# Two shared side tiles to the end, second hidden in the block sums' space, and a new order

## The chip, the cores and the metric

The kernel runs on one core of a Trainium2 chip. The core has TensorE (PE, matmuls and weight loads), VectorE (DVE), ScalarE (ACT), GpSimd (POOL) and a queue (SP) that starts the DMAs. PE writes to PSUM, eight banks of 128 x 512 f32. The metric is device microseconds of one execution; the median of 3 runs of the kernel before is 963.83 (962.95 to 963.94).

## What is computed

```python
scores = (q @ k.T) / sqrt(64)          # B=8, H=8, S=576, D=64
scores = where(block_i >= block_j, scores, -1e9)   # blocks of 64
attn   = softmax(scores) @ v
x      = attn.transpose(0, 2, 1, 3).reshape(4608, 512)
out    = relu(x @ w_in) ** 2 @ w_out   # w_in 512x2048, w_out 2048x512
```

All is f32 to the caller. Both large products run in f16: each operand is split into a high and a low f16 part, and three matmuls (high x high, high x low, low x high) make one product.

## The kernel before

The work is cut into 4048 tasks with names; every instruction is issued by one helper, so all rows of a trace have line 331 and are told apart by their tiles.

**Attention.** 40 "passes" of two heads each (i = 0 to 39). Passes 0 to 7 take only the first rows, 8 to 15 the rest of the same heads, 16 to 39 all rows. A full pass has three groups of rows. For each group: `A` scores on PE into a side tile (two PSUM banks), `B` the row maximum on DVE (`nmx`, read from the side tile), `C` the exponential on ACT (`p`, read from the side tile, which is free behind it), `S` and `R` row sums and inverses, `H` and `L` the f16 high and low parts of the probabilities (`p_rows`), `T` a DMA that transposes them (`p_turned`). Then `G` multiplies with v on PE (`px`) and `X` evicts `px` to x.

**The rest.** x is taken in 12 chunks of 384 tokens in the order 0, 1, 2, 4, 3, 5, 7, 6, 8, 10, 9, 11. A chunk is normed (`nq`, `hb`, `xm`) and split to f16 (`xt_all`). The first three chunks go in 16 units each: `ph` (12 matmuls of 128x384 into `pair`), then `pos`, `sqr`, `top`, `rem` (relu, square, high, low), the result in `hidden`. The other nine go in four groups each, of seven products of blocks (`p1 p2 p6 p5 p7 p4 p3`, 12 matmuls of 128x192 each) into two PSUM banks X and B, read by `c11`, `a11` and so on into `r`; `p3` is the last product, `a12` its reader on DVE. The groups need sums of blocks of w_in (`t0_0` to `t3_17`, in `turned_w`). Behind each chunk come the output products `po{chunk}_{m}_{f}` (three matmuls of 128x512, 48 per m) with the eviction `ob` and the store. The weights come as int64 words (`r` raw w_in, `z` raw w_out); `bits`, `prelu`, `join`, `max`, `cast` and `low` make scaled f16 parts of them.

**The order.** One string, `ORDER`, lists all tasks in the order in which they are issued, with a letter for the engine where there is a choice (`D`, `A`, `P`). `Plan.run` issues them, and each engine's queue keeps that order. `Plan.add` says what a task needs, which ring of buffers it takes a slot of, and which it frees.

**PSUM.** Before pass 14 (`ALONE`): side0 and side1 (two banks each), pair0 and pair1 (a bank each), and `ps_x`, two banks for everything that is called `x`, `px` among it. From pass 14 on side1 and pair1 are given up for three banks `group`, a ring of three for the groups' X and B. Output products of late chunks take pair0 alone (`po`). The raw pieces of w_out lie where `PLACES` says, in parts of `w2`, `hidden` and `turned_w`.

Of the kernel before, what the change touches and what calls it, by code (L numbers as in the profile page):

```python
# [8 lines left out]
F32 = mybir.dt.float32  # L9
# [8 lines left out]
PSUM = bass.MemoryType.PSUM  # L18
# [90 lines left out]
D7:P F5:A nq0_0 bits0_7 C8_1 E6 F6:A bits0_5 w0d0 w0e0 E7 F7:A r13 r14 G4 keys10 X4_0:A clear join0_4 hb0_0 S8_1 G5 cast0_0:A D8_0:A X5_0:A G6 join0_6
A9_0 xm0_0 G7 X6_0:A Q4:A bits0_11 E8_0_0 h0_0 X7_0:A R8_1 low0_0 max0_11 B9_0 Q6:A bits0_8 Q5:A cast0_1:P E8_0_1 Q7:A F8_0_0:A bits0_13 max0_14 nq1_0  # L110
max0_12 prelu0_7 max0_8 C8_2 F8_0_1:A hb1_0 load10 join0_5 load8 D8_1:A max0_9 S8_2 E8_0_2 F8_0_2:A R8_2 A9_1 E8_1_0 xm1_0 bits0_9 l0_0 C9_0 h1_0 B9_1
D8_2:A E8_1_1 l1_0 bits0_10 F8_1_0:A F8_1_1:A max0_13 A9_2 E8_2_0 E8_2_1 z0 prelu0_8 r15 max0_15 z1 F8_2_0:A F8_2_1:A join0_7 z2 z3 bits1_0 prelu0_9
S9_0 R9_0 C9_1 D9_0:A w0a1 prelu0_10 ph0_0 w0b1 low0_1 cast0_2:P B9_2 w0c1 join0_8 G8_1 low0_2 S9_1 R9_1 C9_2 join0_9 w0d1 ph0_1 prelu0_11 cast0_3:A
w0e1 bits0_12 w0e A10_1 D9_1:A bits1_3 A10_0 ia0_0 E9_0_0 bits1_1 pos0_0 low0_3 prelu0_12 join0_10 S9_2 join0_11 R9_2 cast0_4:P pos0_1 z4 B10_0 X8_1:A
bits0_14 F9_0_0:A sqr0_1 D9_2:A low0_4 join0_12 ph0_2 prelu0_13 top0_1:D pos0_2 prelu0_14 C10_0 E9_0_1 cast0_5:P ph0_3 E9_0_2 F9_0_2:A B10_1 ph0_4
F9_0_1:D bits1_2 C10_1 pos0_3 low0_5 E9_2_0 S10_0 bits0_15 join0_14 R10_0 prelu0_15 join0_13 D10_0:D cast0_6:P sqr0_3 prelu1_0 pos0_4 low0_6 prelu1_1
keys11 join1_0 cast0_7:P A10_2 E9_1_0 F9_1_0:A A11_0 S10_1 join0_15 sqr0_0 B10_2 F9_2_0:A low0_7 ph0_5 cast0_8:P E9_2_1 prelu1_2 top0_0:D B11_0
max1_0:A ph0_6 top0_3:A pos0_5 join1_2 R10_1 C10_2 S10_2 low0_8 E9_1_1 F9_2_1:A rem0_3 ph0_7 R10_2 F9_1_1:A cast0_9:D load9 A11_1 sqr0_4 G9_1 rem0_1
z5 low0_9 B11_1 D10_1:A sqr0_2 pos0_7 bits1_5 pos0_6 cast0_10:P C11_0 D10_2:D low0_10 load11 prelu1_3 E10_0_0 sqr0_5 S11_0 top0_2:D X9_1:A F10_0_0:A
C11_1 E10_0_1 top0_5:D max1_2:D join1_1 load12 cast0_11:P F10_0_1:A E10_0_2 F10_0_2:A R11_0 sqr0_7 max1_1:D bits1_4 S11_1 sqr0_6 A11_2 E10_1_0  # L120
F10_1_0:A load13 E10_1_1 A12_0 low0_11 z6 top0_4:D cast0_12:P z7 E10_2_0 B11_2 F10_1_1:A R11_1 join1_3 rem0_4 prelu1_4 max1_3:D D11_0:A low0_12 ph0_8
top0_7:A C11_2 F10_2_0:A E10_2_1 F10_2_1:A rem0_0 prelu1_5 D11_1:A join1_4 ph0_9 pos0_9 cast0_13:P B12_0 A12_1 prelu1_6 G10_1 S11_2 C12_0 pos0_8 z8
prelu1_7 join1_5 R11_2 max1_5:A rem0_7 X10_1:A A12_2 E11_0_0 D11_2:D low0_13 B12_1 cast0_14:P F11_0_0:A max1_4:D vals12 ph0_10 C12_1 B12_2 E11_0_1
E11_0_2 bits1_6 join1_6 A13_0 low0_14 S12_1 F11_0_1:A prelu1_8 max1_6:D F11_0_2:A sq0_1_0 bits1_7 join1_7 S12_0 bits1_8 rem0_2 R12_1 join1_8 E11_2_0
# [273 lines left out]
def attention_moe_kernel(ctx: ExitStack, tc: tile.TileContext, qk1, v1, qk, ks, vm, vt, w_in, w_out, out):  # L398
# [387 lines left out]
    def side_of(t, group):  # L786


        if t["i"] >= ALONE:
            return 0  # L790
# [1233 lines left out]
```

## Time and profile before

| | before |
|---|---|
| median of 3 runs | 963.83 us |
| the profiled execution | 963.4 us |
| its span | 961.6 us |
| PE busy | 936.5 us, 97% |
| DVE busy | 764.7 us, 80% |
| ACT busy | 638.6 us, 66% |
| POOL busy | 267.9 us, 28% |

The span is what the profile covers; 1.8 us of the execution lie outside it. A busy PE is not yet PE at its best: its rows overlap by the pipeline's depth, so how fast matmuls go is read from start to start. PE's idle time is short and lies in few places, so a table by stretches is read first, and then the timelines of these places. Rows of DVE and ACT matter where PE waits for them.

### The profile page before, as it was taken

What the parts mean: (1) busy time and instruction counts of PE and PEld (TensorE: products, weight loads), DVE (VectorE), ACT (ScalarE), POOL (GpSimd) and SP (SyncE); (2) the same over time, 40 slices, a digit from 0 to 9 for tenths busy, and PEclk for the clock granted to TensorE, in tenths of its full rate; (3) what the DMA queues carried; (4) which work ended last, traced back from release to release, by engine and by line L of the source; (5) the groups of instructions that cost most, each with busy time, mean ns of one, the idle gap of its engine ahead of it and who ended that gap; (6) DMA issues with size and microseconds to landing.
All of it is one profiled execution on the core that took longest, in us unless ns stands there. A gap on an engine that the chain in (4) does not pass through costs nothing.

```text
span 961.6 us, 21188 instructions
## 1 busy us (share of the span) xinstructions
PE 936.5 (97%) x8145; PEld 602.6 (63%) x8145; DVE 764.7 (80%) x1703; ACT 638.6 (66%) x1585; POOL 267.9 (28%) x371
## 2 busy tenths in 40 slices
PE   8899899999998999999999999999999999999998
PEld 5455444545554784785676675686675675596675
DVE  6999997789899997899879788698879777656331
ACT  6999986765895786885475576678657555365330
POOL 4586401222255541224032032031112012011110
PEclk9999999999999999999999999999999999999999
DMA  9915477656855318435665346564473354400001
GB/s 358 399 63 186 153 163 164 139 135 136 188 115 121 83 51 190 104 63 118 124 155 123 78 107 112 119 150 94 86 176 84 74 117 81 91 13 12 12 1 45
DMA packets 221650, 114.93 MB, mean 120 GB/s; under 512 B 195290, under 2 KB 203756, under 8 KB 221548
## 3 DMA queue, kind: packets, MB, share of 16 engines
q1 hardware_dynamic: 221548, 113.57, 48.5%
q8 instruction: 64, 1.05, 0.4%
q14 instruction: 38, 0.31, 0.1%
HBM read 58.21 MB, written 9.46 MB: 70 GB/s over the span
## 4 chain that ended last, share of the span: by engine, by line
PE 81%; DVE 10%; ACT 3%; POOL 2%; issue 2%; DMA 2%; SPq 0%; DVEq 0%; ACTq 0%; POOLq 0%
PE pair L331 40%; PE group L331 24%; PE side L331 8%; PE px L331 6%; DVE nmx L331 2%; DVE p_rows L331 2%; PE po L331 2%; DVE w L331 2%; DMA w<-in_w_in 1%; POOL w L331 1%; DVE xt_all L331 1%; DVE stw L331 1%; DMA vraw<-in_v 1%; ACT p L331 1%; DVE x L331 1%
## 5 line engine op out<-in xcount | busy, mean ns | idle before, releaser
L331 PE MATMUL pair<-w,hidden 128*128 128x512 f16 (+1 forms) x1680 | 382.1, 376 | 1.0 <-DVE ob L331 0.9
L331 PEld LDWEIGHTS <-hidden 128*128 128x128 f16 x1776 | 168.5, 98 | 179.0 <-issue 11.7
L331 PEld LDWEIGHTS <-w 128*128 128x128 f16 x2304 | 200.4, 98 | 56.9 <-issue 10.3
L331 ACT ACTIVATE p<-side,nmx 128x576 f32<-128x576 f32 (+8 forms) x264 | 140.1, 541 | 94.3 <-DVE nmx L331 45.6
L331 POOL TENSOR_TENSOR hidden<-r,hidden 128x384 f16<-128x384 f32 x103 | 104.0, 1020 | 219.7 <-ACT hidden L331 204.6
L331 PE MATMUL group<-xt_all,w 128*128 128x192 f16 x1728 | 161.8, 247 | 0.8 <-DVE xt_all L331 0.5
L331 DVE SCALAR_TENSOR_TENSOR p_rows<-p,rs,p_rows 128x64 f16<-128x64 f32 (+7 forms) x264 | 147.2, 578 | 11.0 <-ACT p_rows L331 8.8
L331 DVE TENSOR_REDUCE nmx<-side 128x1 f32<-128x192 f32 (+8 forms) x288 | 123.4, 481 | 27.2 <-PE side L331 26.4
L331 POOL TENSOR_SCALAR sm<-sm 128x2 f32<-128x2 f32 (+2 forms) x104 | 34.5, 332 | 333.2 <-ACT p L331 316.0
L331 PE MATMUL group<-xt_all,turned_w 128*128 128x192 f16 x1296 | 122.8, 246 | 0.0
L331 PEld LDWEIGHTS <-turned_w 128*128 128x128 f16 x1296 | 108.1, 98 | 14.2 <-issue 4.9
L331 ACT ACTIVATE p_rows<-p,rs 128x64 f16<-128x64 f32 (+11 forms) x173 | 90.3, 554 | 31.8 <-DVE rs L331 21.2
L331 ACT ACTIVATE r<-group,rescale 128x384 f32<-128x384 f32 x111 | 63.7, 579 | 69.2 <-PE group L331 61.5
L331 ACT ACTIVATE r<-r 128x384 f32<-128x384 f32 x177 | 90.9, 523 | 20.0 <-DVE r L331 17.7
L331 ACT CAST hidden<-r 128x384 f16<-128x384 f32 x172 | 84.7, 507 | 28.8 <-DVE r L331 19.1
L331 DVE SCALAR_TENSOR_TENSOR r<-group,rescale,r 128x384 f32<-128x384 f32 x108 | 65.9, 613 | 45.8 <-PE group L331 32.5
L331 PE MATMUL side<-qk 64*64 64x512 f32 (+2 forms) x480 | 97.0, 498 | 3.5 <-ACT p L331 3.4
L331 PE MATMUL pair<-xt_all,w 128*128 128x384 f16 x576 | 98.9, 326 | 1.1 <-DVE xt_all L331 0.7
L331 PE MATMUL side<-ks,qk 64*64 64x192 f32 (+4 forms) x576 | 91.9, 424 | 0.0
L331 PE MATMUL px<-p_turned,v 128*64 128x384 f16 (+5 forms) x1168 | 66.8, 269 | 0.3 <-ACT p_turned L331 0.3
L331 PEld LDWEIGHTS <-v 128*64 128x64 f16 x1128 | 48.5, 110 | 21.5 <-issue 11.3
L331 DVE TENSOR_TENSOR hidden<-r,hidden 128x384 f16<-128x384 f32 x89 | 51.3, 579 | 7.5 <-ACT hidden L331 7.1
(154 smaller groups left out, 1060.3 us busy)
## 6 DMA issues: line engine op xcount, KB each, us to landing
qk<-in_qk SPq DMA_DIRECT2D x32, 576.0 KB
ks<-in_ks SPq DMA_DIRECT2D x32, 320.0 KB
vraw<-in_vm SPq DMA_DIRECT2D x30, 256.0 KB
w<-in_w_out SPq DMA_DIRECT2D x10, 512.0 KB
out<-ob SPq DMA_DIRECT2D x17, 256.0 KB
w<-in_w_in SPq DMA_DIRECT2D x8, 512.0 KB
out<-ob SPq DMA_DIRECT2D x26, 128.0 KB
hidden<-in_w_in SPq DMA_DIRECT2D x6, 512.0 KB
```

The lines of the kernel that those rows point to most:

```text
L331: i = make(*a, **k)
```

## The change

`ps_x`, the `group` banks and the switch at pass 14 go. The eight banks are now side0, side1, pair0, pair1, single0, single1 from the start to the end. Scores take the two side tiles in turn through one ring `s`, and the products with v of passes from 16 on (and others that aren't "whole") take a whole side tile of the same ring, one half for each of their two parts. The groups' X and B take pair0 and pair1, swapped from group to group. single0 and single1 are the ring `x` early on; later single0 is `y` (norms, v's scales), single1 is `po`. The second chunk's hidden lies in `turned_w`'s space, so the block sums from `t{n}_3` on come only after the second chunk's output products with those parts. `PLACES` puts other raw pieces of w_out in turned_w. `ORDER` is new as a whole, with other letters too: of the weights' casts ACT has 14 for 12, DVE 10 for 7, POOL 8 for 13; of the row sums DVE 36 for 29, POOL 12 for 19; of the high parts of p_rows ACT 167 for 155, DVE 97 for 109. PE's matmuls are the same in number and shape.

```diff
 PLACES = (
     {f: ("w2", 7 - f) for f in range(8)} | {f: ("hidden", f - 8) for f in range(8, 14)} | {14: ("turned", 0), 15: ("turned", 1)},
-    {0: ("w2", 7), 1: ("w2", 6), 2: ("w2", 5), 4: ("w2", 4)}
-    | {5: ("w2", 7), 6: ("w2", 6), 7: ("w2", 5), 9: ("w2", 7), 10: ("w2", 6), 11: ("w2", 7)}
-    | {3: ("turned", 2), 8: ("turned", 3), 12: ("turned", 4)},
+    {3: ("w2", 7), 4: ("w2", 6), 5: ("w2", 5), 6: ("w2", 4)}
+    | {7: ("w2", 7), 8: ("w2", 6), 9: ("w2", 7), 10: ("w2", 6), 11: ("w2", 7)}
+    | {0: ("turned", 2), 1: ("turned", 3), 2: ("turned", 4)},
 )
...
-p0 A0 B0 C0 p1 A1 A2 B1 S0 R0 C1 r0 max0_0 prelu0_0 B2 D0:P S1 R1 C2 r1 prelu0_1 bits0_0 A3 p2 D1:P E0 F0:A A4 r2 B3 C3 E1 max0_1 A5 bits0_1 S2
+p0 p1 r0 r1 p2 A0 r2 r3 A1 r4 B0 C0 p3 B1 r5 C1 S0 A2 R0 r6 D0:D r7 max0_0 prelu0_0 A3 S1 r8 bits0_0 R1 B2 r9 D1:P E0 prelu0_1 keys8 B3 C2 r10 bits0_1
...
-    ps_x = ctx.enter_context(tc.tile_pool(name="ps_x", bufs=2, space=PSUM))
-    sides = [ps_b.tile([P, 1024], F32, name="side0")]
-    pairs = [ps_b.tile([P, 512], F32, name="pair0")]
-    early = ExitStack()
-    ps_e = early.enter_context(tc.tile_pool(name="ps_e", bufs=1, space=PSUM))
-    sides.append(ps_e.tile([P, 1024], F32, name="side1"))
-    pairs.append(ps_e.tile([P, 512], F32, name="pair1"))
-    homes = {"mm": pairs, "po": pairs[:1]}
-    turns_of = dict(mm=0, po=0, g=0)
+    bank = lambda name, n: ps_b.tile([P, 512 * n], F32, name=name)
+    pairs, singles = ([bank(f"{name}{n}", 1) for n in range(2)] for name in ("pair", "single"))
+    homes = {"s": [bank(f"side{n}", 2) for n in range(2)], "mm": pairs, "x": singles, "y": singles[:1], "po": singles[1:]}
+    turns_of = {ring: 0 for ring in homes}
...
-        if ring not in homes:
-            early.close()
-            ps_g = ctx.enter_context(tc.tile_pool(name="ps_g", bufs=1, space=PSUM))
-            homes[ring] = [ps_g.tile([P, 512], F32, name=f"group{n}") for n in range(3)]
         turns_of[ring] += 1
         return homes[ring][(turns_of[ring] - 1) % len(homes[ring])]
...
+    hidden_too = turned_w.rearrange("p i z b k -> p (i z b k)").rearrange("p (f z s) -> p f z s", f=NF, z=2)
...
-            ps = box["ps"] = sides[side_of(t, group)]
+            ps = box["ps"] = bank_of("s")
...
-        full = ps_x.tile([P, 512], F32, tag="x", name=f"px_{u}_{g}")
+        if t["whole"]:
+            full = bank_of("x")
+        else:
+            if "home" not in t:
+                t["home"] = bank_of("s")
+            full = t["home"][:, 512 * (1 - g) :]
...
+    def hidden_of(ck):
+
+        return hidden_too if turn_of.index(ck) == 1 else hidden
...
         def bank(name):
-            box[name] = bank_of("g")[:, :CH]
+            box[name] = pairs[(g + (name == "B")) % 2][:, :CH]
...
-            {"s0": 1, "s1": 1, "mm": 2, "x": 2, "p32": 2, "ks": 2, "v16": 2, "g": 3, "po": 1, "qk": 2, "r": 8, "hb": 2, "ob": 3, "dg": 1, "top": 1}
+            {"s": 2, "mm": 2, "x": 2, "y": 1, "p32": 2, "ks": 2, "v16": 2, "g0": 1, "g1": 1, "po": 1, "qk": 2, "r": 8, "hb": 2, "ob": 3, "dg": 1, "top": 1}
...
-                    ("p1", lows("01") + weights + ([f"p2{ck}_{g - 1}"] if g else []), ("g",)),
-                    ("p2", [f"p1{k}"], ("g",)),
+                    ("p1", lows("01") + weights + ([f"p2{ck}_{g - 1}"] if g else []), (f"g{g % 2}",)),
+                    ("p2", [f"p1{k}"], (f"g{1 - g % 2}",)),
...
-                add(f"a12{k}", "DVE", 545, [f"p3{k}", f"c12{k}"], r, step("a12"), frees=[(f"p2{k}", "g")])
+                add(f"a12{k}", "DVE", 545, [f"p3{k}", f"c12{k}"], r, step("a12"), frees=[(f"p2{k}", f"g{1 - g % 2}")])
...
+                if x == 3:
+                    after += [f"po{turn_of[1]}_{m}_{4 * n + e}" for m in range(3) for e in range(4)]
...
-                        f"G{i}", "PE", 2186 if len(gs) > 1 else 1844, back + [f"vl{i}"], rank + 6, both_parts, ("x",) * len(gs),
+                        f"G{i}", "PE", 2186 if len(gs) > 1 else 1844, back + [f"vl{i}"], rank + 6, both_parts, ("s",),
```

How the order moves, at three places. First PE at the last group of scores of pass 21 and the first of pass 22 (`qk_1`, `qk_2` and `ks_1`, `ks_2` are queries and keys of these groups, `side` their tile). Before, some 100 rows lie between the two:

```order
L331 MATMUL pair_76<-w_108,hidden 128x512
L331 MATMUL side_75<-qk_1_0_3202 64x512 x2
L331 MATMUL side_75<-ks_1_0_3204 64x64 x2
L331 MATMUL side_75<-ks_1_0_3204,qk_1_0_3202 64x448 x2
L331 LDWEIGHTS v_3_0_0_3464
...
L331 MATMUL pair_76<-w_108,hidden 128x512
L331 MATMUL side_75<-qk_2_0_3693 64x320 x2
L331 MATMUL side_75<-ks_2_0_3695,qk_2_0_3693 64x256 x2
L331 MATMUL side_75<-qk_2_0_3693 64x64 x2
L331 MATMUL side_75<-ks_2_0_3695,qk_2_0_3693 64x192 x2
```

After, in the same place:

```order
L331 MATMUL single_75<-w_104,hidden 128x512
L331 MATMUL side_77<-qk_1_0_2963 64x512 x2
L331 MATMUL side_77<-ks_1_0_2965 64x64 x2
L331 MATMUL side_77<-ks_1_0_2965,qk_1_0_2963 64x448 x2
L331 MATMUL side_76<-qk_2_0_3517 64x320 x2
L331 MATMUL side_76<-ks_2_0_3519,qk_2_0_3517 64x256 x2
L331 MATMUL side_76<-qk_2_0_3517 64x64 x2
L331 MATMUL side_76<-ks_2_0_3519,qk_2_0_3517 64x192 x2
L331 LDWEIGHTS turned_w
```

The two groups used one tile with other work between them; now they stand back to back and have a tile each.

Second DVE at the same place (`nmx` is the row maximum of those scores, `p_rows` the low parts of pass 20's probabilities). Before:

```order
L331 SCALAR_TENSOR_TENSOR p_rows<-p_3_1_0_7_3604,rs_1_0_7_3718,p_rows 128x128
L331 TENSOR_SCALAR m_2_0_3734<-pm_2_0_3646 128x2
L331 TENSOR_TENSOR turned_w<-t_AluOpType.subtract_3639,turned_w 128x2x256
L331 SCALAR_TENSOR_TENSOR p_rows<-p_3_1_0_7_3604,rs_1_0_7_3718,p_rows 128x384
L331 SCALAR_TENSOR_TENSOR p_rows<-p_3_1_0_7_3604,rs_1_0_7_3718,p_rows 128x512
L331 TENSOR_REDUCE nmx_1_0_8_3748<-side_75 128x1 x2
L331 TENSOR_SCALAR nmx_1_0_8_3748<-nmx_1_0_8_3748 128x2
```

After:

```order
L331 TENSOR_SCALAR ob_1_3724<-single_75,uv_3466 128x512
L331 TENSOR_REDUCE nmx_1_0_8_3739<-side_77 128x1 x2
L331 TENSOR_SCALAR nmx_1_0_8_3739<-nmx_1_0_8_3739 128x2
L331 TENSOR_TENSOR t_AluOpType.subtract_3756<-w_103 128x512
L331 SCALAR_TENSOR_TENSOR p_rows<-p_3_1_0_7_3656,rs_1_0_7_3685,p_rows 128x128
L331 TENSOR_REDUCE nmx_2_0_4_3770<-side_76 128x1 x4
L331 TENSOR_SCALAR nmx_2_0_4_3770<-nmx_2_0_4_3770 128x4
L331 TENSOR_TENSOR xt_all<-x_93,xt_all 128x768
L331 SCALAR_TENSOR_TENSOR p_rows<-p_3_1_0_7_3656,rs_1_0_7_3685,p_rows 128x384
```

The row maximum stood behind the two wide lows of `p_rows`; now both row maxima stand ahead of them.

Third PE at the hand-over from the third to the fourth group of chunk 4 (`group` and `pair` are the groups' banks, the weights are parts of `xt_all`). Before, the next group's first product, into `group_3837`, stands ahead of the old group's last, into `group_3839`:

```order
L331 LDWEIGHTS turned_w
L331 MATMUL group_3838<-xt_all,turned_w 128x192
L331 LDWEIGHTS w_107
L331 MATMUL group_3837<-xt_all,w_107 128x192
...
L331 LDWEIGHTS w_107
L331 MATMUL group_3839<-xt_all,w_107 128x192
```

After, one output product stands between the last matmul of the old group's last product and the next group's first:

```order
L331 LDWEIGHTS w_103
L331 MATMUL pair_73<-xt_all,w_103 128x192
L331 LDWEIGHTS hidden
L331 MATMUL single_75<-w_104,hidden 128x512
...
L331 LDWEIGHTS w_103
L331 MATMUL pair_73<-xt_all,w_103 128x192
```

There were three banks in turn, so the next group opened a free one; now it opens the bank `pair_73` that the old group has just filled.

## Rows read from the trace of the kernel before

**Rows 1.** The page: span, and each engine's busy time.

```profile
span 961.6 us, 21188 instructions
PE 936.5 (97%) x8145; PEld 602.6 (63%) x8145; DVE 764.7 (80%) x1703; ACT 638.6 (66%) x1585; POOL 267.9 (28%) x371
```

**Rows 2.** Stretches: us, busy PE, PEld, DVE, ACT, POOL, clock, DMA share, GB/s.

```profile
0.00:20.00 20.00, 15.21 (x143) 11.19 (x145) 13.06 (x51) 13.81 (x54) 9.09 (x23) 1.00 0.91 346
20.00:120.00 100.00, 88.62 (x658) 50.28 (x655) 95.69 (x205) 94.75 (x236) 61.70 (x82) 0.97 0.58 209
120.00:300.00 180.00, 180.00 (x1315) 92.90 (x1314) 157.58 (x359) 130.76 (x327) 48.10 (x67) 1.00 0.66 147
300.00:320.00 20.00, 16.88 (x156) 11.18 (x155) 18.31 (x30) 11.25 (x27) 10.74 (x11) 0.91 0.49 90
320.00:820.00 500.00, 498.85 (x4753) 339.54 (x4751) 417.73 (x945) 333.61 (x835) 118.22 (x169) 1.00 0.50 110
820.00:961.60 141.60, 136.95 (x1134) 97.56 (x1128) 62.33 (x118) 54.38 (x108) 20.09 (x22) 1.00 0.13 30
```

**Rows 3.** Timeline of PE, 303 to 318: start, us, what, [idle before, releaser].

```profile
303.06 0.65 PE L331 MATMUL side<-qk 64*64 64x512 f32 x2
...
311.58 0.49 PE L331 MATMUL side<-qk 64*64 64x320 f32 x2 [3.07 <-ACT p L331]
...
312.50 1.24 PE L331 MATMUL pair<-w,hidden 128*128 128x512 f16 x3
313.52 3.44 PE L331 MATMUL group<-xt_all,w 128*128 128x192 f16 x24
316.80 1.15 PE L331 MATMUL group<-xt_all,turned_w 128*128 128x192 f16 x12
```

**Rows 4.** Timelines of POOL, DVE and ACT at the same place.

```profile
305.11 2.92 POOL L331 TENSOR_TENSOR _AluOpType.subtract<-_AluOpType.subtract,w 128x512 f32<-128x512 f32 x2
...
305.50 3.08 DVE L331 SCALAR_TENSOR_TENSOR p_rows<-p,rs,p_rows 128x384 f16<-128x384 f32 x2
308.50 1.27 DVE L331 TENSOR_REDUCE nmx<-side 128x1 f32<-128x576 f32 x2
...
310.08 0.74 ACT L331 ACTIVATE p<-side,nmx 128x576 f32<-128x576 f32 x1 [2.97 <-DVE nmx L331]
```

**Rows 5.** Groups by line and form, DVE: busy, mean ns of one | idle before.

```profile
L331 DVE SCALAR_TENSOR_TENSOR p_rows<-p,rs,p_rows 128x512 f16<-128x512 f32 x28 | 22.6, 806 | 0.0
...
L331 DVE SCALAR_TENSOR_TENSOR p_rows<-p,rs,p_rows 128x384 f16<-128x384 f32 x28 | 19.1, 682 | 1.1 <-ACT p_rows L331 1.0
```

**Rows 6.** Timeline of PE, two groups of scores in one side tile.

```profile
156.19 0.65 PE L331 MATMUL side<-qk 64*64 64x512 f32 x2
...
157.22 3.41 PE L331 MATMUL pair<-w,hidden 128*128 128x512 f16 x15
160.56 0.65 PE L331 MATMUL side<-qk 64*64 64x512 f32 x2
```

**Rows 7.** Timeline at 350: last product into a group's bank, and its reader.

```profile
350.72 1.40 PE L331 MATMUL group<-xt_all,w 128*128 128x192 f16 x15
...
352.16 0.62 DVE L331 SCALAR_TENSOR_TENSOR r<-group,rescale,r 128x384 f32<-128x384 f32 x1 [0.30 <-PE group L331]
```

**Rows 8.** Groups by line and form: the weights' casts on three engines.

```profile
L331 POOL TENSOR_SCALAR w<-w,wsc 128x512 f16<-128x512 f32 x12 | 22.7, 1893 | 14.0 <-DVE w L331 13.7
...
L331 DVE TENSOR_SCALAR w<-w,wsc 128x512 f16<-128x512 f32 x7 | 3.4, 481 | 0.1
...
L331 ACT ACTIVATE w<-w,wsc 128x512 f16<-128x512 f32 x11 | 7.9, 719 | 4.2 <-DVE w L331 4.1
```

**Rows 9.** Timelines of DVE and PE at 826: one output bank in turn.

```profile
826.05 0.81 DVE L331 TENSOR_SCALAR ob<-pair,uv 128x512 f32<-128x512 f32 x1 [0.98 <-PE pair L331]
...
826.92 1.45 PE L331 MATMUL pair<-w,hidden 128*128 128x512 f16 x6 [0.90 <-DVE ob L331]
```

**Rows 10.** Timeline of DVE at the end.

```profile
957.89 0.54 DVE L331 TENSOR_SCALAR ob<-pair,uv 128x256 f32<-128x256 f32 x1 [3.65 <-PE pair L331]
```

More of the change, by code (lines that the diff above doesn't have):

```diff
@@ L109 @@
[L109 to L112, printed above, removed]
@@ L709, in turned @@
         def turned():
-            pm = box["pm"] = ps_x.tile([P, 512], F32, tag="x", name=f"pm_{u}")
+            pm = box["pm"] = bank_of("x" if pair[0]["i"] == WHOLE else "y")
             nc.tensor.transpose(pm[:2, :P], box["st"], ident)
@@ L784, in scores @@
                 nc.tensor.matmul(ps[D * h : D * h + D, o], q[rs], keys[rs, k], start=True, stop=True)
-    def side_of(t, group):
-        if t["i"] >= ALONE:
-            return 0
-        n = [j for g, _, _ in t["groups"] for j, _ in g[:1]].index(group[0][0])
-        return (t["i"] * len(t["groups"]) + n) % 2
     def rows(t, group):
@@ L1361, in products @@
                 ring = out_ring(ck, n)
-                bank = ps_x.tile([P, 512], F32, tag="x", name=f"po_{ck}_{n}") if ring == "x" else bank_of(ring)
-                box["po"] = bank[:, :w]
+                box["po"] = bank_of(ring)[:, :w]
             for i, (z, k) in enumerate(((0, 0), (0, 1), (1, 0))):
@@ L1618, in norm @@
             step = lambda n: lambda *q: box["s"][n](*q)
-            add(f"hb{k}", "DVE", 680 if big == 1 else 950, frees, rank, start, ("hb",), frees=[(f"nq{k}", "x")])
+            add(f"hb{k}", "DVE", 680 if big == 1 else 950, frees, rank, start, ("hb",), frees=[(f"nq{k}", x_of_norm(b, g))])
             add(f"xm{k}", "DVE", 160 + 0.985 * size, [f"hb{k}"], rank, step("scaled"), frees=[(f"hb{k}", "hb")])
@@ L1688, in square @@
             add(
-                f"nq{k}", "PE", 165 * len(halves), [f"sa{k}_{a}" for a in halves], rank, sums, ("x",),
+                f"nq{k}", "PE", 165 * len(halves), [f"sa{k}_{a}" for a in halves], rank, sums, (x_of_norm(b, g),),
                 frees=[(f"sq{k}_{a}", "sq") for a in halves],
@@ L1740, in moe @@
                 add(f"a22{k}", "DVE", 545, [f"p5{k}", f"c22{k}"], r, step("a22"))
-                add(f"a12{k}", "DVE", 545, [f"p3{k}", f"c12{k}"], r, step("a12"), frees=[(f"p2{k}", "g")])
-                add(f"c21{k}", {"ACT": 469, "DVE": 533}, 0, [f"p4{k}"], r, step("pos"), ("r",), frees=[(f"p1{k}", "g")])
+                add(f"a12{k}", "DVE", 545, [f"p3{k}", f"c12{k}"], r, step("a12"), frees=[(f"p2{k}", f"g{1 - g % 2}")])
+                add(f"c21{k}", {"ACT": 469, "DVE": 533}, 0, [f"p4{k}"], r, step("pos"), ("r",), frees=[(f"p1{k}", f"g{g % 2}")])
                 for name in ("11", "21", "22", "12"):
@@ L1760, in moe @@
                 early = UR[0] + UR[1] * f
-                over = [f"po{prev}_{m}_{f}" for m in range(3)] if ck else []
+                over = [f"po{turn_of[n - 2] if n == 2 else prev}_{m}_{f}" for m in range(3)] if ck else []
+                if n == 1:
+                    held = {14: (0, 4096), 15: (4096, 8192)}, {g: (8192 + 4096 * g, 12288 + 4096 * g) for g in range(3)}
+                    meets = lambda a, e: a < 1536 * (f + 1) and e > 1536 * f
+                    over = [f"{x}{v}_{g}" for v in range(2) for g, at in held[v].items() if meets(*at) for x in ("join", "max")]
+                    over += [f"low{v}_{NF - 1}" for v in range(2) if meets(20480 + 2048 * v, 22528 + 2048 * v)]
                 if not ck:
```

456 lines of the change are left out of this document (232 added, 224 removed).

## The prediction

> **What bounds the kernel now.** I read the totals first: TensorE (PE) is busy 936.5 of 961.6 us and no other engine passes 80% [rows 1]. PE's work is the same after the change (8145 matmuls of the same shapes), so all that a new order can win is PE's idle time, a slow clock, or the time PE loses between matmuls. Then the table by stretches [rows 2]: PE is idle 4.79 us in the first 20, 11.38 in 20 to 120, nothing to 300, 3.12 in 300 to 320, 1.15 in the 500 us behind that, and 4.65 from 820 on. So there are three places to look at. In 20 to 120 VectorE (DVE) is busy 95.69 and ScalarE (ACT) 94.75 of 100: this stage hangs on these two, not on PE. At 300 to 320 one wait does it. The end is a chain behind the last matmul.
>
> The timeline of the second place [rows 3] shows it: PE's scores of pass 22 wait 3.07 us until ACT has read those of pass 21, since from pass 14 on all scores share one side tile. They were written at 303.06, but their row maximum on DVE starts only at 308.50, because two lows of p_rows stand ahead of it in DVE's queue; these take 3.08 together while GpSimd (POOL) runs a pair of subtractions for 2.92 [rows 4], where the two forms take 0.682 and 0.806 on the mean [rows 5]. Behind the wait the clock of this stretch falls to 0.91 on the mean [rows 2]: 24 group matmuls take 3.28 to the next row's start where 0.083 each (15 in 1.40, 12 in 1.15) makes 2.00, and three output matmuls take 1.02 where 0.217 each (15 in 3.41, 6 in 1.45) makes 0.65 [rows 3, 6, 7, 9]. The place costs 3.07 + 1.28 + 0.37 = 4.7.
>
> **The change part by part.** I start from the profiled execution's 963.4 (span 961.6 and 1.8 outside it).
>
> *Two side tiles to the end, and the new order around pass 21: -4.7.* In the new list pass 21's last and pass 22's first scores stand back to back in two tiles, and pass 21's row maximum stands ahead of the lows of pass 20. The wait as it was can't come again there, and with PE busy the clock has no gap to fall behind. Bounds: all of it goes (4.7), or, if DVE is as late with another instruction, nothing does. I take all, since both its causes (the single tile, the place behind the lows) are changed.
>
> *Fewer switches on PE: -1.2.* Between 157.22 and the scores at 160.56 stand 15 matmuls of 0.217, 3.26 of 3.34 us: going over to 64-row work costs some 0.09 [rows 6]. From pass 14's scores to the end I count 75 such entries into runs of scores or products with v in the old list and 62 in the new: 13 x 0.09 = 1.2. Bounds 0 to 1.2: a switch may hide in a wait.
>
> *Two banks for the groups, not three: +1.2.* Now the first product of a group goes into the bank that DVE still reads as the last result of the group before. The trace has no such wait (three banks hid it). Its parts: DVE starts 0.04 behind the last matmul's end and takes 0.62 [rows 7]; the drain behind the last matmul's slot is 1.40 - 15 x 0.083 = 0.16, and 0.06 from DVE's end to PE's start (826.05 + 0.81 to 826.92 [rows 9]): 0.88 with a free DVE. The nearest whole case, an output bank read by DVE between two of PE's matmuls, makes PE wait 0.90 [rows 9]. Between last and next first product the new list holds 0.65 us of other PE work once, 0.97 to 1.03 four times, 1.29 three times, at least 1.57 in the other 19 of 27 hand-overs (matmul counts by the pitches above). One wait of 0.23 is certain then; one more DVE instruction of 0.62 in front makes it 0.85, the next four 0.5 each and the three of 1.29 some 0.2: 0.85 + 4 x 0.5 + 3 x 0.2 = 3.4. Bounds 0.2 to 27 x 0.88 = 24 (no cover at all); I take 1.2, nearer to the free DVE, because over 320 to 820 DVE is idle 82 of 500 us [rows 2].
>
> *The side ring shared with products of v: +1.0.* These took banks of their own before; now each takes a whole side tile until both its evictions are done, so a score group may have to wait for an eviction. A score group holds its tile some 4 us: in the old trace two groups in the one tile were 4.37 apart without a wait [rows 6]. The new list has 12 places where the PE work between one use of the ring and the next but one is under 5.3 us (shortest 2.76 and 2.87, around pass 14's first products; then 4.4 and more); the old had four, of which one waited, 3.07. At that share the cost is 12 x (3.07 + 1.65)/4 = 14 with its clock; with none late it is 0. I take 1.0: the two short ones are short of 4 by 1.2 together if scores hold the tile, and less where evictions do.
>
> *The first 120 us: -0.8.* Ahead of pass 14's first scores the lists hold the same PE work (100.1 against 100.7 us, by the trace's durations) and 273 instructions on DVE for 274, 233 on ACT for 234, 98 on POOL for 96. Over the whole list five casts of weights leave POOL, two go to ACT and three to DVE: 5 x 1.893 off a queue that is 38% idle here, 2 x 0.719 onto ACT and 3 x 0.481 onto DVE [rows 8]. The loads of w_out's raw pieces and the first of w_in's stand earlier in SP's queue, past loads of q and k, at a DMA share of 0.91 [rows 2], which cuts both ways: the first scores come later, the weights sooner. Casts and lows end two or three PE tasks sooner. The second chunk's hidden in the block sums' space doesn't bring that chunk forward: in both lists only five of its units stand ahead of the first output product, for these need no new space. DVE's 4.31 idle in 20 to 120 is the most this order can win or, mirrored, lose: -4.3 to +4.3. I take -0.8.
>
> A row bears on this: DVE's lows were slow beside POOL (3.08 for 1.49). The Trainium skill, "SBUF — State Buffer", section "Who interferes with whom", says that a DVE operation with two SBUF inputs and a POOL operation that reads SBUF exclude each other, and that the later one blocks fully until the first ends; the trace agrees here (the pair's 2.92 covers the two lows). By that rule alone every cast that leaves POOL would free DVE for up to 1.89 us, which is the first rival's result.
>
> *Unchanged:* the 0.90 wait at 826.92 (in both lists the next output's first matmul stands directly behind the last one's, on one bank) [rows 9], and the end: the last copy of 0.54 at 957.89 and its store, 3.7 us in all [rows 10].
>
> **Sum:** 963.4 - 4.7 - 1.2 + 1.2 + 1.0 - 0.8 = 958.9. The profiled execution lies 0.4 under the median of the runs, 963.83; I leave it at 958.9.
>
> **The rivals.** *First: the early stage gets shorter too.* With five casts less on POOL, DVE's two-input lows and joins in 20 to 120 run undisturbed (they overlap POOL's casts of 1.89 [rows 8]); if that frees the whole 4.31 of idle and waiting, the time is 958.9 + 0.8 - 4.3 = 955.4. For it: both engines at 95% set this stage. Against: three casts go to DVE itself, and POOL gets other work (its count rises from 96 to 98).
>
> *Second: the change doesn't do what it says.* The stall at 308 goes, but the sums of w_in, drawn together into fewer microseconds, and one bank less make as much new waiting, spread over the groups: 3.4 from the banks in place of 1.2, and 2 to 3 more on the ring: 958.9 + 2.2 + 2 = 963.1. For it: half the price of my banks' term is a guess. Against: DVE is less full after 320.
>
> *Third: slower, by the shared side ring.* Twelve short returns are three times as many as before; a wait such as that at 311 cost 4.7 with its clock. From the second such wait on it is decided: 958.9 + 2 x 4.7 = 968.3. The place is passes 14 to 27, where DVE is busy 18.31 of 20 at worst [rows 2] and a row maximum or an eviction may stand behind lows. Against: there are two tiles, so a late reader is first covered by the other one.
>
> **How the numbers follow.** My forecast, 955.5 to 961.9: 0.49. First rival, below 955.5: 0.13. Second, 961.9 to 965.8: 0.19. Third, above 965.8: 0.19. A measurement of this kernel can tell about 0.2%, 1.9 us, from no change, so faster is below 961.9: 0.49 + 0.13 = 0.62, same 0.19, slower 0.19. The range 952.5 to 967.0 leaves out the far end of the first rival (0.03) and most of the third (0.15). The forecast's own range is 955.5 to 961.9.
>
> **What would show it.** In the table by stretches the piece that holds pass 22's scores should have PE idle under 0.5 and the clock at 1.00. The waits of PE's first group product on DVE's r should sum to about 1, those of side matmuls on ACT's p or x to about 1; if either is above 4, that term was the failed step. The first 120 us should hold PE idle of 15 to 16, and the 0.90 in front of an output's first matmul should stand. I am wrong if the stall has come back at another pass, with the clock down behind it, or if the early stage moved by more than 4 us either way.

## The result, and the profile after

The changed kernel takes 954.57 us (median of 4 runs, 953.6 to 955.89) against 963.88 (962.95 to 964.57): ratio 0.9905, 95% interval 0.9888 to 0.9922, so 9.3 us faster. The forecast was 958.9, its range 952.5 to 967.0. The direction is right and the time lies in the range, but the gain is nearly twice the one forecast: the time is below the forecast's own range (955.5 to 961.9), where the first rival (0.13) stood. The profiled execution is the slowest of the four, 955.9.

The page after, span and busy time:

```profile
span 954.1 us, 21192 instructions
PE 932.0 (98%) x8145; PEld 604.3 (63%) x8145; DVE 760.7 (80%) x1716; ACT 634.8 (67%) x1583; POOL 248.4 (26%) x357
```

PE's busy time fell by 4.5 us [rows 1] with the same 8145 matmuls. Waits that went away don't count in that; PE does the same work faster, by its clock or by its order. The table by stretches, with 320 to 420 apart (columns as in [rows 2]):

```profile
0.00:20.00 20.00, 15.21 (x143) 11.21 (x144) 13.71 (x46) 12.97 (x47) 9.17 (x22) 1.00 0.92 351
20.00:120.00 100.00, 90.05 (x674) 50.68 (x673) 95.72 (x217) 97.83 (x248) 51.27 (x79) 1.00 0.65 219
300.00:320.00 20.00, 20.00 (x222) 14.89 (x221) 18.13 (x35) 13.34 (x35) 9.87 (x13) 1.00 0.35 67
380.00:420.00 40.00, 37.95 (x371) 28.37 (x370) 29.56 (x70) 29.78 (x73) 6.13 (x10) 0.96 0.60 117
420.00:820.00 400.00, 398.34 (x3749) 271.14 (x3747) 323.90 (x744) 257.53 (x646) 86.94 (x125) 1.00 0.50 110
```

The stretch of the old stall is full and at full clock. A new hole of 2.05 us with a lowered clock stands at 380 to 420. What PE waits for from 120 on, by the view of waits (total, times, longest), before:

```profile
PE side L331 <- ACT p L331: 3.4, 2, 3.1
PE group L331 <- DVE xt_all L331: 0.5, 1, 0.5
PE group L331 <- DVE r L331: 0.2, 1, 0.2
```

(and the 0.9 in front of an output), and after:

```profile
PE side L331 <- DMA qk<-in_qk: 2.7, 2, 2.0
PE single L331 <- DVE ob L331: 0.9, 1, 0.9
```

So this view has no wait on the groups' banks from 120 on, and none on the side ring's readers; two waits for a load of q and k, which the forecast doesn't have; and the 0.90 in front of an output, as said. It leaves out very short waits. One of these is a hand-over between groups, the third one shown in the section on the change:

```profile
335.09 0.81 PE L331 MATMUL single<-w,hidden 128*128 128x512 f16 x3
335.96 2.14 PE L331 MATMUL pair<-xt_all,w 128*128 128x192 f16 x24
```

Three output matmuls (0.65) stand there, and the next group's first product starts 0.87 after their start: 0.22 of waiting. The wait for the load, in PE's timeline and then in SP's queue:

```profile
394.77 1.15 PE L331 MATMUL pair<-xt_all,w 128*128 128x192 f16 x12
397.88 0.76 PE L331 MATMUL side<-qk 64*64 64x320 f32 x4 [1.96 <-DMA qk<-in_qk]
...
399.94 1.46 PE L331 MATMUL single<-w,hidden 128*128 128x512 f16 x3
401.19 2.88 PE L331 MATMUL pair<-xt_all,w 128*128 128x192 f16 x24
403.91 0.33 PE L331 MATMUL single<-sq,ones_bf 128*128 128x384 bf16 x1
```

```profile
388.76 1.53 SPq L331 DMA_TRANSPOSE p_turned<-p_rows  x1
390.34 2.06 SPq L331 DMA_DIRECT2D out<-ob  x2
392.44 0.59 SPq L331 DMA_DIRECT2D qk<-in_qk  x1
```

The load of pass 26 is issued 5.4 us ahead of its scores, behind a transpose and a store. Two more costs stand behind the wait. The scores take 2.06 to the next row's start (0.92 in [rows 3]), three output matmuls 1.25 for 0.65, 24 group matmuls 2.72 for 2.00. With the wait that is 4.4 us. A part of it is a second wait: the queries have come, but the weight loads (PEld) that need the keys `ks` still wait for their DMA. The rest is the clock, which is at half. The weight loads at this place and at pass 37, and the stretch of the low clock:

```profile
398.73 0.14 PEld L331 LDWEIGHTS side<-ks,qk 64*64 64x64 f32 x2 [0.66 <-DMA ks<-in_ks]
...
704.78 0.14 PEld L331 LDWEIGHTS side<-ks,qk 64*64 64x64 f32 x2 [0.50 <-DMA ks<-in_ks]
```

```profile
399.20:402.80 3.60, 3.60 (x20) 2.15 (x17) 2.58 (x9) 0.00 (x0) 0.00 (x0) 0.53 0.67 185
```

At pass 37 PE waits 0.75 for the queries, and its scores take 1.60 for 0.92 because of the keys: 1.4 in all, with the clock at 1.00. So of the 4.4 some 2.0 are the first wait, 0.7 the keys and 1.7 the clock.

Where PE got faster is seen in the timeline of the pair of scores that the forecast speaks of, each group's first row and the row behind the pair:

```profile
300.30 0.65 PE L331 MATMUL side<-qk 64*64 64x512 f32 x2
...
301.21 0.44 PE L331 MATMUL side<-qk 64*64 64x320 f32 x2
...
302.09 1.16 PE L331 MATMUL pair<-xt_all,turned_w 128*128 128x192 f16 x12
```

The two groups take 302.09 - 300.30 = 1.79 us together. With other work behind each they take 1.95: the second 0.92 (311.58 to 312.50 [rows 3]) and the first 1.03 (the first experiment below shows its rows). Start to start, the pairs take 703 + 1080 or 909 + 986 ns, where groups apart take 920 + 1027 or 1027 + 1032. From pass 14's first scores on there are 25 pairs after, and none before (the one tile can't hold two groups).

### The profile page after: what moved, and what is told of

The parts are those of the page before. It is cut to its first block, busy times and chain, and to the rows that moved or that the text cites. A ratio compares the mean times of both kernels' runs of the same rounds, so it can differ in the third digit from the quotient of the medians.

```text
span 954.1 us, 21192 instructions
## 1 busy us (share of the span) xinstructions
PE 932.0 (98%) x8145; PEld 604.3 (63%) x8145; DVE 760.7 (80%) x1716; ACT 634.8 (67%) x1583; POOL 248.4 (26%) x357
## 4 chain that ended last, share of the span: by engine, by line
PE 84%; ACT 4%; DMA 1%; DVE 1%; SPq 1%; issue 0%; ACTq 0%
PE pair L331 38%; PE single L331 32%; PE side L331 13%; ACT r L331 1%; ACT p L331 1%; DMA ks<-in_ks 1%; SPq L331 1%; DMA qk<-in_qk 0%; DMA raw<-in_w_out 0%; DVE r L331 0%; ACT p_rows L331 0%; ACT p_turned L331 0%; ACT wt L331 0%; ACT raw L331 0%; ACT hidden L331 0%
## 5 line engine op out<-in xcount | busy, mean ns | idle before, releaser
L331 PE MATMUL single<-w,hidden 128*128 128x512 f16 (+1 forms) x1488 | 333.4, 373 | 0.9 <-DVE ob L331 0.9
L331 PE MATMUL pair<-xt_all,w 128*128 128x192 f16 (+1 forms) x2304 | 260.7, 267 | 1.3 <-ACT r L331 1.1
L331 ACT ACTIVATE r<-pair,rescale 128x384 f32<-128x384 f32 x151 | 87.5, 582 | 93.6 <-PE pair L331 90.2
L331 DVE SCALAR_TENSOR_TENSOR p_rows<-p,rs,p_rows 128x128 f16<-128x128 f32 (+6 forms) x264 | 142.2, 562 | 9.1 <-ACT p_rows L331 7.8
L331 DVE TENSOR_REDUCE nmx<-side 128x1 f32<-128x576 f32 (+8 forms) x288 | 123.2, 480 | 22.3 <-PE side L331 21.8
L331 PE MATMUL pair<-xt_all,turned_w 128*128 128x192 f16 x1296 | 124.5, 246 | 0.2
L331 DVE SCALAR_TENSOR_TENSOR r<-pair,rescale,r 128x384 f32<-128x384 f32 x108 | 66.2, 613 | 61.4 <-PE pair L331 40.8
L331 ACT ACTIVATE p_rows<-p,rs 128x128 f16<-128x128 f32 (+9 forms) x183 | 94.5, 552 | 19.6 <-DVE rs L331 12.4
L331 PE MATMUL side<-p_turned,v 128*64 128x384 f16 (+3 forms) x1128 | 61.8, 265 | 0.0
L331 ACT ACTIVATION_READ_ACCUMULATOR p<-side,nmx 128x1 f32 x264 | 54.2, 205 | 0.0
```

The costliest lines, as they stand in the source:

```text
L331: i = make(*a, **k)
```

## The experiments

All were timed in 5 rounds beside the kernel before. The first two sessions' time of before is 964.0 and 964.2, the last one's 963.8.

**The pairs taken apart.** In the kernel after, PE's next task is put between the two groups of each pair, as here:

```diff
-A21_2 ob2_1:D sq114_0:A t3_12:P A22_0 out2_1 B21_2 T20_1_1 p64_0 t3_13:D
+A21_2 ob2_1:D sq114_0:A t3_12:P p64_0 A22_0 out2_1 B21_2 T20_1_1 t3_13:D
```

> The kernel after, but with the 25 pairs of score groups that stand back to back on PE (from pass 14 on) taken apart: the PE task behind each pair now stands between its two groups. Same tiles, same work on every engine. Theory (pairs): in the trace after, a pair costs 703 + 1080 or 909 + 986 ns where two single groups cost 920 + 1027 or 1027 + 1032, so 0.165 us is saved inside a pair, and one entry of 0.094 besides: 25 x 0.26 = 6.5 us lost, 961 us. Rival (the forecast's price, an entry alone): 25 x 0.094 = 2.3 us lost, 957 us. Second rival (the gain is elsewhere): within 1 us of the kernel after.

Measured: 962.21, ratio 0.9986 (0.9975 to 0.9997), 7.6 us above the kernel after. The timeline shows the groups at their single price, 303.56 to 304.59:

```profile
303.56 0.65 PE L331 MATMUL side<-qk 64*64 64x512 f32 x2
...
304.59 1.17 PE L331 MATMUL pair<-xt_all,turned_w 128*128 128x192 f16 x12
305.69 0.49 PE L331 MATMUL side<-qk 64*64 64x320 f32 x2
```

PE's waits from 120 on barely differ (2.4 on loads for 2.7). So nearly all of it is in how matmuls follow each other: 25 x 0.26 = 6.5 was expected, the price of an entry alone (2.3) falls. The two traces can be set side by side place by place, from the last start ahead of a pair to the first start behind the moved task: 22 of the 25 places take 0.25 to 0.27 us more, the other three 0.41 to 0.57, with new waits of 0.10 to 0.25. One pair is worth 0.26 us.

**The row maximum moved up in the kernel before.**

```diff
-fd22 t2_12:D L21_1_1 po2_1_15 A21_2 L21_1_0 B21_2 t0_13:P
+fd22 t2_12:D po2_1_15 A21_2 B21_2 L21_1_1 L21_1_0 t0_13:P
```

> The kernel before, with one move: the row maximum of pass 21's last scores stands ahead of the two wide lows of p_rows on DVE, not behind them (PE's order is the same, the one side tile stays). Theory (the stall at 308 is worth what its rows say): the wait of 3.07 falls under 0.5 and the clock of 300 to 320 stays at 1.00, so 4.7 us less than before, about 959.2 us. Rival: the lows, and what follows them, are late instead and PE waits there, within 1 us of before, 963 to 964 us.

Measured: 961.52, ratio 0.9971 (0.996 to 0.9981), 2.5 us less: half. The old place, and the two that follow it, then the stretch:

```profile
309.81 0.49 PE L331 MATMUL side<-qk 64*64 64x320 f32 x2 [0.95 <-ACT p L331]
...
322.79 1.15 PE L331 MATMUL group<-xt_all,w 128*128 128x192 f16 x12 [0.60 <-DVE r L331]
...
328.09 1.15 PE L331 MATMUL group<-xt_all,w 128*128 128x192 f16 x12 [0.97 <-DVE r L331]
```

```profile
300.00:320.00 20.00, 19.05 (x184) 12.01 (x182) 19.41 (x32) 11.94 (x28) 13.26 (x11) 1.00 0.52 94
```

The clock stays at 1.00, but the single tile still costs 0.95, and DVE, which has the two lows to do now, is late twice for a group. Both theories were half right: the clock's share is won, the wait's is mostly given back within 20 us.

**The row maximum put back in the kernel after.** The base here, and for the hand-overs and the old cast letters below, is the kernel after with the load of pass 26 moved up (its run stands further down, 953.56).

```diff
-A22_0 out2_1 B21_2 T20_1_1 p64_0 t3_13:D po2_2_0 C21_2 L21_1_2
+A22_0 out2_1 T20_1_1 H21_1_1:A H21_1_0:A L21_1_1 L21_1_0 B21_2 p64_0 t3_13:D po2_2_0 C21_2 L21_1_2
```

(The two highs and the two lows that move up here stood further down; that part is not shown.)

> The kernel after with pass 26's load moved up, and with the old order of DVE at pass 21: the high and low parts of p_rows, the two wide lows among them, stand ahead of the row maximum of pass 21's last scores again; the two side tiles stay. Theory (the second tile alone covers a late row maximum): PE has no wait over 0.5 between 300 and 320 and the time is within 0.7 us of 953.6. Rival (the place of the row maximum is what took the stall away): PE waits 2 us or more for a side tile or for a group's reader, and the time is 2 to 5 us above, 955.5 to 958.5.

Measured: 959.56, ratio 0.9955 (0.9943 to 0.9968), 6.0 above its base. The timelines of DVE, ACT and PE there, and the stretch:

```profile
304.04 0.62 DVE L331 SCALAR_TENSOR_TENSOR p_rows<-p,rs,p_rows 128x384 f16<-128x384 f32 x1 [2.33 <-ACT p_rows L331]
307.01 0.75 DVE L331 SCALAR_TENSOR_TENSOR p_rows<-p,rs,p_rows 128x512 f16<-128x512 f32 x1 [2.34 <-DMA p_turned<-p_rows]
307.67 1.28 DVE L331 TENSOR_REDUCE nmx<-side 128x1 f32<-128x576 f32 x2
```

```profile
309.25 0.74 ACT L331 ACTIVATE p<-side,nmx 128x576 f32<-128x576 f32 x1 [4.63 <-DVE nmx L331]
...
310.60 0.58 ACT L331 ACTIVATE r<-pair,rescale 128x384 f32<-128x384 f32 x1
```

```profile
311.23 0.27 PE L331 MATMUL pair<-xt_all,turned_w 128*128 128x192 f16 x1 [2.50 <-ACT r L331]
313.19 1.92 PE L331 MATMUL pair<-xt_all,turned_w 128*128 128x192 f16 x11 [1.70 <-DVE xt_all L331]
```

```profile
300.00:320.00 20.00, 15.80 (x119) 9.36 (x118) 12.63 (x26) 9.13 (x25) 7.29 (x7) 0.83 0.22 42
```

No score waits for a side tile: the second tile does cover that. But ACT keeps its order: the eviction of a group's product stands behind the late exponential, and PE waits for that. It is a harder case than the old order, since the lows have to wait for their own inputs here (2.33 and 2.34 of idle DVE). What it shows is that with a row maximum as late as this the tile alone isn't enough; its place is needed too.

**Hand-overs between groups laid bare.** Seven times, as here:

```diff
-p39_1 po9_0_2 po9_0_3 p19_2
+p39_1 p19_2 po9_0_2 po9_0_3
```

(PE's tasks alone are shown; those of other engines keep their place).

> The kernel after with pass 26's load moved up, and with seven hand-overs between groups of products laid bare: the output products between the last product of a group and the first of the next (1 to 8 of them) stand behind that first product, which opens the bank that was filled last. Theory (the forecast's price: 0.88 us a hand-over with a free DVE, hidden by what stands between): 7 x 0.88 = 6.2 us more, 959.8 us, as seven waits on DVE's r. Rival (DVE is behind by one more operation at these places): 7 x 1.5 = 10.5 more, 964. Second rival (PE's queue or the banks hide it): under 2 us more.

Measured: 963.93, ratio 0.9999 (0.999 to 1.0008), 10.4 above its base. PE's waits from 120 on, and two of the places:

```profile
PE pair L331 <- DVE r L331: 5.3, 7, 1.0
PE pair L331 <- DVE xt_all L331: 3.2, 1, 3.2
```

```profile
846.62 1.15 PE L331 MATMUL pair<-xt_all,w 128*128 128x192 f16 x12 [0.71 <-DVE r L331]
...
866.87 0.26 PE L331 MATMUL pair<-xt_all,w 128*128 128x192 f16 x1 [0.71 <-DVE r L331]
870.33 1.92 PE L331 MATMUL pair<-xt_all,w 128*128 128x192 f16 x11 [3.20 <-DVE xt_all L331]
872.05 3.19 PE L331 MATMUL single<-w,hidden 128*128 128x512 f16 x7
```

Six of the seven wait 0.71 and with the drain of 0.16 cost 0.87 each, the seventh 1.17: 6.4 together, for 6.2 expected. The total looks like the first rival's 10.5, but it is not that: at 866.87 the product came too early for its own input (3.2, and a slow stretch behind it). The price in the forecast was right, and the output products in between hide all of it in the kernel after but the 0.22 at 335.96.

**Two moves in the first 80 us of the kernel before.**

```diff
-nq1_0 max0_12 prelu0_7 max0_8 C8_2 F8_0_1:A hb1_0 load10 join0_5 load8 D8_1:A max0_9 S8_2 E8_0_2
+max0_12 prelu0_7 max0_8 C8_2 F8_0_1:A load10 join0_5 load8 D8_1:A max0_9 S8_2 E8_0_2 nq1_0 hb1_0
...
-cast0_10:P C11_0 D10_2:D low0_10 load11 prelu1_3 E10_0_0 sqr0_5 S11_0 top0_2:D X9_1:A
+cast0_10:P X9_1:A C11_0 D10_2:D low0_10 load11 prelu1_3 E10_0_0 sqr0_5 S11_0 top0_2:D
```

> The kernel before, with two moves in the first 80 us: the squared sums of x (nq1_0, and its reader hb1_0) stand behind the transposes E8_0_2 on the two banks of the x ring, and the eviction X9_1 stands ahead of the exponential C11_0 on ACT. These take away the waits of 2.15 at 36 us and 1.82 at 74 us, behind which the clock fell (0.69 over 40 to 45, 0.86 over 70 to 80; 3.3 us of work lost by the clock). Theory (these waits and the clock make the early stage longer): 4 to 7 us less, 957 to 960 us. Rival (DVE and ACT at 95% set this stage, PE's waits there cost nothing): within 1.5 us of before, and the waits come back elsewhere before 120 us.

Measured: 963.84, ratio 1.0001 (0.9992 to 1.0009): nothing. The waits came back a task later:

```profile
37.29 0.80 PE L331 MATMUL nq<-sq,ones_bf 128*128 128x192 bf16 x4 [1.04 <-ACT p_turned L331]
...
76.50 0.66 PE L331 MATMUL pt<-ident,p_rows 128*128 128x128 f32 x4 [2.45 <-ACT p_turned L331]
```

From 20 to 120 PE is idle for 10.42 us, for 11.38 before [rows 2]:

```profile
20.00:120.00 100.00, 89.58 (x656) 50.58 (x653) 95.19 (x204) 94.73 (x236) 61.76 (x83) 0.95 0.57 207
```

So the moves shifted PE's waits and took hardly any of them away. That fits the rival, by which DVE and ACT set this stage; that a wait of PE costs nothing there is not shown, since the waits are not gone.

**The casts' engines, in both lists.** In the kernel after the old letters, in the kernel before the new ones:

```diff
-cast0_0:P cast0_1:A cast0_2:A ... cast0_4:A cast0_5:D ... cast0_10:D ... cast0_15:D
+cast0_0:A cast0_1:P cast0_2:P ... cast0_4:P cast0_5:P ... cast0_10:P ... cast0_15:P
```

(shown: the new list. Ten casts of the second matrix, `cast1`, change between ACT and DVE besides.)

> The kernel after with pass 26's load moved up (the run on the load, 953.6 us), and with the old letters of the weights' casts: POOL takes 13 again instead of 8, ACT 12 and DVE 7; ten more of the casts change between ACT and DVE. Nothing else moves. Theory (the first rival of the prediction, casts on POOL hold up DVE's two-input operations in the first 120 us): in the trace DVE's lows of the weights take 763 ns after and 820 before, 18 of them, and the kernel after is some 2 us ahead by the first scores of pass 14; the old letters should give that back, 955 to 956.5 us, with the lows above 800 ns. Rival (the new order of the early tasks did it, not the engine of the casts): within 0.7 us of 953.6.

> The kernel before with one edit: the weights' casts take the letters of the kernel after (POOL 8 instead of 13, ACT 14, DVE 10; ten more change between ACT and DVE). Nothing moves in the list. The converse run gave 4.3 us back to the old letters in the new list. Theory (the letters by themselves free the early stage): 2 to 4 us less than before, 960 to 962 us, with the first scores of pass 14 at least 1.5 us earlier than 126.7. Rival (each list suits its own letters, and what the converse run lost is the misfit): within 1 us of before or above it, 963 to 967 us.

Measured: the old letters in the new list 957.81, ratio 0.9933 (0.9921 to 0.9946), 4.3 above its base; the new letters in the old list 965.99, ratio 1.0019 (1.0011 to 1.0028), 2.2 slower than before. The lows of the weights on DVE before 127 us, first of the kernel before, then of the kernel after, then of the new list with the old letters, then of the old list with the new ones:

```profile
L331 DVE SCALAR_TENSOR_TENSOR w<-w,wsc 128x512 f16<-128x512 f32 x18 | 14.8, 820 | 0.5 <-POOL w L331 0.5
```

```profile
L331 DVE SCALAR_TENSOR_TENSOR w<-w,wsc 128x512 f16<-128x512 f32 x18 | 13.7, 763 | 0.2 <-POOL w L331 0.2
```

```profile
L331 DVE SCALAR_TENSOR_TENSOR w<-w,wsc 128x512 f16<-128x512 f32 x16 | 12.7, 794 | 3.4 <-POOL w L331 3.1 <-ACT w L331 0.4
```

```profile
L331 DVE SCALAR_TENSOR_TENSOR w<-w,wsc 128x512 f16<-128x512 f32 x18 | 14.6, 810 | 0.6 <-POOL w L331 0.5
```

The old letters don't slow the lows by much (794 for 763); DVE stands idle 3.1 for POOL's casts. The new letters in the old list hardly make them faster (810 for 820 before), and over the whole run win nothing.

PE's order is the same within each pair of kernels, so the same matmul can be timed in both traces. With the old letters the new list is behind by 1.8 us at the first scores of pass 14 (126.96 for 125.15), and by 4.7 from 147 on. With the new letters the old list is ahead by 2.9 at 87 us and 2.6 at 100, but by only 0.2 at the first scores of pass 14 (126.48 for 126.67), and behind by 1.5 at 152. (One profiled execution each; two kernels with the same list up to 100 us differ there by up to 0.8.) So the new letters do win time early in both lists, but the old list loses it again before pass 14, and in both runs a good part of the total comes between 127 and 152, where the ten other casts stand. The runs don't part these from the five that leave POOL, so they don't tell what the gain of the early stage is.

**Loads and one output bank.** First the load of pass 26 alone:

```diff
-T24_0_0 T24_0_1 T24_1_0 out4_1 load26 T24_1_1
+T24_0_0 T24_0_1 load26 T24_1_0 out4_1 T24_1_1
```

(the tasks on SP's queue).

> The kernel after, with the load of pass 26's q and k issued before the transpose T24_1_0 on SP's queue instead of behind it and a store. Theory (the wait of 1.96 at 395 in the profiled execution is the queue's, and the clock behind it costs 2.4 more): no wait on that load, clock 1.00 over 380 to 420, a profiled run near 951.5 us, and a median of 1 to 2.5 us less than the kernel after, since some of its executions show no lowered clock at all: 952 to 953.5 us. Rival (the load is slow because of what else the DMA engines carry): the wait stays, time unchanged.

Measured: 953.56, ratio 0.9891 (0.9878 to 0.9903), 1.0 below the kernel after. The wait is gone and the clock of 380 to 420 full:

```profile
380.00:420.00 40.00, 40.00 (x421) 31.00 (x420) 33.69 (x79) 31.41 (x76) 6.78 (x12) 1.00 0.68 141
```

Its profiled span is 951.1 for 954.1; the place itself is 4.5 shorter, but at pass 37 PE now waits 1.86 for its load. Not every execution of the kernel after had the clock down, so the median gains less. From 392.4 to 397.9 the DMA share of the kernel after is 1.06, all engines full; here the load is issued at 382.29, at a share of 0.62 (382 to 390). The run doesn't part the place in the queue from what the DMA engines carry at that time. Then two versions with more of it; the first moves pass 37's load past a transpose and two stores, adds two pairs and gives chunk 10's last output product a side tile, the second moves that load further up, past four loads of v too, and adds no pairs (its order is shown):

```diff
-ring: "y" if n == len(turn_of) - 1 and m % 2 else "po"
+ring: "y" if n == len(turn_of) - 1 and m % 2 else "s" if (ck, m) == (10, 2) else "po"
...
-T35_1_0 vals36 T35_1_1 out6_1 out6_0 load37 load38
+T35_1_0 load37 vals36 T35_1_1 out6_1 out6_0 load38
```

> The kernel after with pass 26's load moved up and four moves more: the load of pass 37's q and k stands ahead of a transpose and two stores on SP's queue, the scores A25_2 and A34_1 stand right behind A25_1 and A34_0 (two pairs more, 27), and the output product of chunk 10's last part opens a side tile instead of the bank that is still read. Theory: no wait at pass 37 (1.9 in the last profile, and 0.7 of clock), two pairs at 0.26, and the 0.9 at 815 gone with its drain of 0.16: 953.6 - 2.5 - 0.5 - 1.0 = 949.6 us. Rival (the loads are late by the DMA engines, not by their place; the pairs make later tasks wait): 952.5 to 953.6.

Measured: 952.02, ratio 0.9875 (0.9862 to 0.9888). That misses the 949.6 and lies under the rival's 952.5. The load's wait is gone; a product with v waits instead for the transpose that was passed:

```profile
700.56 1.75 PE L331 MATMUL side<-p_turned,v 128*64 128x384 f16 x28 [1.30 <-DMA p_turned<-p_rows]
```

The two added pairs win nothing either: PE waits 0.67 for a group's reader on ACT behind the first, and 0.54 for an exponential behind the second, which the run above doesn't have.

> The kernel after with pass 26's load moved up, the load of pass 37 ahead of four loads of v on SP's queue (so that it passes no transpose that is wanted soon), and the output product of chunk 10's last part in a side tile; no pairs are added. Theory (late waits are a load's or a transpose's place on SP's queue): no wait at pass 37 on load or transpose (1.9 and 1.3 in the two profiles before), no 0.9 at 815: 953.6 - 1.9 - 0.7 - 1.06 = 949.9 us. Rival (moving one transfer up makes another late there, since the DMA engines are full at 700 us): 951.5 to 953 us.

Measured: 950.32, ratio 0.9858 (0.9845 to 0.9871), as expected (949.9), the fastest here: 13.5 below the kernel before and 4.3 below the one after. All that PE waits for from 120 us on:

```profile
PE side L331 <- DMA p_turned<-p_rows: 0.3, 1, 0.3
```

## Why the prediction was right, and where it was not

The sum of the forecast, from 963.4, against the profiled execution after, 955.9 (each from the traces, start to start):

| term | forecast | measured |
|---|---|---|
| the stall at 308 and its clock | -4.7 | -4.9 |
| switches on PE | -1.2 | -5.1 |
| two banks for the groups | +1.2 | +0.2 |
| waits on the side ring | +1.0 | 0 |
| the first 120 us | -0.8 | some -2 |
| loads of q and k late | not in it | +5.8 |
| other short waits of PE from 120 on | not in it | -0.8 |
| the end | 0 | -0.5 |
| sum | -4.5 | -7.3 of -7.5 |

The other short waits are 1.8 us in five places before and 1.1 in five after, with the drain before each. The end was to stay as it was; from the start of the last copy to the end of the span it takes 3.20 after (950.86 to 954.06) for 3.73 before, and 3.20 or 3.21 in every other run of the new list. Why is not shown.

That the time lies in the range is in part luck. The switches won 3.9 more than forecast, and the late loads, which the sum does not have, took 5.8. The last run above, in the same order but for two loads and one output bank, stands at 950.32, below the range.

The stall went as said, with its clock. That it took both the second tile and the row maximum's place stands on two runs: the place alone won 2.5 of 4.7 in the old kernel, and with the tile alone, and the row maximum late, a wait of 2.5 came through ACT. One sign of being wrong that the forecast names, a stall at another pass with the clock down behind it, did appear, at pass 26; its cause is a load and not the shared tile.

The term that was mis-sized is the one called fewer switches. I priced the entry into 64-row work (0.09, 13 fewer: 1.2) and took the score groups themselves as constant. But of a group's 0.92 or 1.03 a second group right behind it, in the other tile, saves some 0.165 us. The trace before could not show two groups back to back in the late passes, since one tile forbids it; the order showed that they would stand so, and I gave that no bounds of its own. 25 x 0.165 = 4.1, and the entries 1.0 more (79 before and 68 after between 120 and 820 us, so 11 at 0.094); taking the pairs apart costs 7.6. Why two groups in a row take less than their sum is not shown; the rows show only that products with v behind a group save nothing.

The two banks cost 0.2, at the one hand-over where the forecast called 0.23 certain; everywhere else the output products in between cover them. The price of a bare hand-over, 0.88, was right (0.87 measured), and the other 1.0 of the term, for a DVE that is late, did not come. The side ring's waits, priced at 1.0 with an upper end of 14, did not come either: no wait on p or x from 120 on. (The sum behind the 1.0 has a slip: 2.76 and 2.87 are short of 4 by 2.4 together, not 1.2.) So the third rival's mechanism isn't there, though the unpriced neighbour of it is: a score group that stands earlier on PE wants its q and k earlier, and SP's queue was looked at for the first 120 us alone. In the old list the first scores of pass 26 stand 84 tasks behind their load and those of pass 37 112; in the new list 21 and 37. That was the step left out, and the lists show it.

The first 120 us: by the first products with v of pass 12 (127.7 before, 122.9 after) and the first scores of pass 14 (126.7, 124.7) the new kernel is ahead by some 2 us. PE is idle 14.7 us there, where 15 to 16 was said. The first rival says why by POOL's casts, and the traces of the two kernels agree with it (lows at 763 for 820, casts 8 for 12). The runs with exchanged letters agree in part: up to pass 14 the old letters cost the new list 1.8, but the new letters win the old one only 0.2 there. The rule of the Trainium skill that stands beside that rival ("SBUF — State Buffer", section "Who interferes with whom") would by itself have freed DVE for every cast that leaves POOL. That rival's mechanism is not shown. What the new order of the first 100 us wins, and by which task, stays open, and so does what PE's waits there cost.

Why the median gains 9.3 and the profile 7.5: the profiled execution is the longest of four. The other three are 0.8 to 2.3 us shorter; the fastest shows no lowered clock (1.00 on the mean, 0.998 in the rest), and moving that load up brings the median to it (953.56 and 953.6). How long the three waited at 395 was not recorded.

## What to carry to other kernels

When a resource is doubled, ask not only which wait goes but which order becomes possible that could not be before, and price what stands at the seam of two like pieces of work by comparing a piece's length behind different neighbours. When work is moved earlier on one engine, walk back along each of its inputs to the queue that loads it. Moving a wait away in a stretch where other engines are full may only bring it back a task later; one where PE is the bound is priced with the clock behind it.

## What the runs showed that I had not expected

Two groups of 64-row scores in a row on PE, in different tiles, take 1.79 us where apart they take 1.95; scores followed by products with v show no such gain (917 against 920 ns). Waits of 1.96 and 3.07 were followed by a clock at half that cost some 1.7 more each, but behind one of 0.95 the clock stayed at 1.00 over its 20 us. And a load 5.4 us ahead of its use was late by 2, at a DMA share of 1.06, while the same load 14 us ahead was not.
